# A new plan for the instruction order of an attention, MoE and SwiGLU kernel: transfer times, matmul kinds, a shared port, later gates, division on ACT too

## The chip, the cores and the metric

The kernel runs on one core of a Trainium2 chip. The metric is the device time of one execution in microseconds (us), lower is better. The engines are PE (TensorE, matmul and transposes), DVE (VectorE), ACT (ScalarE), POOL (GpSimd) and SP (SyncE, which here only issues DMAs).

## What is computed

All arrays are float32. Attention has batch 2, 8 heads, 576 tokens and head size 64, with a causal mask and a decay bias from a cumulative sum of s:

```python
cum = np.cumsum(np.maximum(s, 0.0), axis=-1)
bias = np.minimum(-(cum[..., :, None] - cum[..., None, :]), 0.0)
scores = np.where(causal, -1e9, q @ k.T / 8 + bias)
attn = np.exp(scores - scores.max(-1))
attn = attn / (attn.sum(-1) + 1e-09)
x = (attn @ v)                               # 1152 tokens x 512
p = domain_probs / (domain_probs.sum(-1) + 1e-09)
for e in range(4):                           # 512 -> 1024 -> 512
    y += p[:, e:e+1] * (np.maximum(x @ w1[e], 0) @ w2[e])
g = y @ w_gate                               # 512 -> 1536
out = (g * sigmoid(g) * (y @ w_val)) @ w_out
```

Each float32 matmul behind attention is made of three with split operands (high and low parts in the float32r format).

## The kernel before

**Stages.** Attention comes first, and dense work of the MoE is woven into it. The 16 pairs of heads times two parts of the sequence make 16 entries of `pairs`: pairs 0 to 7 are early (rows 0 to 255 of each head), pairs 8 to 15 late (rows 256 to 575). For each group of a pair, PE makes scores (L511, L516) with the mask added by a matmul (L519); DVE adds the decay bias and takes the row minimum (`least`, L533, since signs are turned); ACT takes the exponential with its sum (`exp`, L542); DVE adds 1e-9 and inverts (`guard`, L548, L549); one engine multiplies the row by that inverse (`norm`, through `scale`, L327: the division); PE transposes the result (`turn`, L587); ACT or DVE copies the transposes into p; PE multiplies by v (`products`, L646); and the result x is kept as a high and a low part (L662). The bias tile of an early pair, dqe, and the two of a late pair, dql and d, are fetched from a scratch array in DRAM, `rows`, to which the cumulative sum was written; pairs 0 and 1 get theirs through PE instead (`pick`, L451). There are three dqe buffers.

**The order.** Nothing is ordered by hand. All work is given to a planner (`Plan`) as tasks with an engine or a choice of engines, a cost in us, dependencies, buffers (`Ring`) and a rank. `Plan.step` takes the task that can start first by the planner's clocks, lowest rank among equals, and emits its instructions then. Each engine runs its instructions in the order emitted. The costs are constants at the top of the file: `COST` and `pe32` for engines, `ISSUE` and `DMA_KB` for a transfer's issue and its bytes, `DRAIN` and `SWITCH` for PE. They fix the order alone: the program waits for what really is not ready. While PE would be idle by the plan, `fill` puts transposes of a unit matrix there (L399, fillers).

**DMAs.** Almost all are issued by SP, in the planned order: k, q and v of the pairs, bias tiles, weights (`raw`, L784), and dps, the gate probabilities of the MoE (`gates`, L1462), which four small DVE operations (L1466 to L1469) normalise.

**Behind attention** (from about 143 us on) PE runs the rest of the MoE and then SwiGLU, with weights and activations split and added by ACT, DVE and POOL.

Of the kernel before, what the change touches and what calls it, by code (L numbers as in the profile page):

```python
# [17 lines left out]
P = 128  # L18
# [10 lines left out]
NSEL = 2  # L29
SWITCH = 0.15  # L30
NPT = 4
DRAIN = 0.3
HELD = 0.3
HELD2 = 1.0
# [9 lines left out]
AW = 1.6  # L44
NORM = "p"
COPY = "av"
# [13 lines left out]
ISSUE = 0.45  # L60
DMA_KB = 0.0028
SPLIT = "apv"
# [5 lines left out]
LOADS = 12  # L68
GRANK = 17
CUM2 = 10  # L70
CUMAT = 14.0
# [5 lines left out]
UMUL = "vp"  # L77
ULOW = "vp"
ENGINE = {"a": "act", "v": "dve", "p": "pool"}

# [34 lines left out]
def pe32(c):  # L115

    return 2 * max(c / 1200 + 0.003, 0.107)
# [7 lines left out]
class Ring:  # L125


    def __init__(self, n):
        self.n, self.ends = n, []
# [6 lines left out]
class Task:  # L136


    def __init__(self, eng, cost, run, deps, take, give, rank):
        self.eng, self.cost, self.run, self.take, self.give, self.rank = eng, cost, run, take, give, rank  # L140
        self.end, self.held, self.then, self.at, self.same = None, [], [], 0.0, {}
        if eng == "dma":
            self.cost, self.moves = cost
        self.missing, self.note = 0, None
        for d in deps:
            if d.end is None:
                self.missing += 1
                d.then.append(self)
            else:
                self.after(d)  # L150
# [10 lines left out]
class Plan:  # L161


    def __init__(self):
        self.clock = {e: 1.9 if e == "act" else 0.6 for e in ("pe", "act", "dve", "pool", "dma", "bus", None)}
        self.ready, self.filler, self.held = [], None, HELD

        self.busy, self.full = [0.0], [False]

    def add(self, eng, cost, run=None, deps=(), take=(), give=(), rank=0.0):  # L170
        t = Task(eng, cost, run, [d for d in deps if d is not None], take, give, rank)
        if not t.missing:
            self.ready.append(t)
        return t

    def start(self, t):

        at = t.at
        for i, r in enumerate(t.take):
            e = r.free(sum(x is r for x in t.take[:i]))  # L180
            if e is None:
                return None
            at = max(at, e + WAIT)
        if not isinstance(t.eng, dict):
            return max(at, t.same.get(t.eng, 0.0), self.clock[t.eng] if t.eng else 0.0), None
        best = None
        for e, cost in t.eng.items():
            x = max(at, t.same.get(ENGINE[e], 0.0), self.clock[ENGINE[e]])
            key = x + AW * cost + (self.held if e == "v" else 0.0)
            if best is None or key < best[0]:  # L190
                best = (key, x, e)
        return best[1:]
# [32 lines left out]
    def step(self, allow=lambda t: True):  # L225

        best = None
        for t in self.ready:
            if (best is None or t.at <= best[0][0]) and allow(t):
                x = self.start(t)  # L230
# [19 lines left out]
        if t.run:  # L250
            t.run(e) if e else t.run()
        t.end = self.run_pe(at, t.cost) if t.eng == "pe" else at + t.cost
        if t.eng == "dma":
            self.clock["dma"] = t.end
            t.end = self.clock["bus"] = max(t.end + 0.65, self.clock["bus"]) + t.moves
        elif t.eng:
            self.clock[t.eng] = t.end
# [13 lines left out]
def attention_moe_swiglu(ctx, tc, q_early, q_late, k, v, s, dp, w1, w2, wg, wv, wo, out):  # L271
# [40 lines left out]
    def any_of(engines, kind, c, run, deps, n=1, **kw):  # L312
        return add(choices(engines, kind, c, n), None, run, deps, **kw)

# [26 lines left out]
    def attention(ap, ps):  # L341
# [22 lines left out]
        def upper():  # L364
# [8 lines left out]
        spread2 = [(tri[lo, 0:P], mask[lo, :]), (tri[hi, lo], mask[hi, hi]), (tri[lo, P:], mask[lo, lo]), (tri[hi, P:], mask[hi, hi])]  # L373
        t_mask = [any_of("v", "copy", P, lambda e, x=x: move(e, *x), t_clear + [t], rank=-96.5)
                  for y, t in ((spread, t_id), (spread2, t_up)) for x in y]
# [45 lines left out]
        def prepare(pi, release):  # L421
# [24 lines left out]
            if pi < NSEL:  # L446
                def pick():
                    bias()
                    tp = ps.tile([P, BANK], F32, name="tp", tag="tp", bufs=2)
                    for j in range(2):  # L450
                        nc.tensor.matmul(tp[:, j * w:j * w + w], ident[:BH, BP * j + m:BP * j + m + 1].to_broadcast([BH, P]),  # L451
                                         sums[:, early], start=True, stop=True)
                    decay[pi, "tp"] = tp
                first = add("pe", 2 * pe32(w), pick, [t_early, t_id], take=[rg, ring("tp")], rank=rank)
                tb = [any_of("a", "bank", 2 * w, lambda e: move(e, decay[pi].rearrange("p j n -> p (j n)"), decay[pi, "tp"]), [first],
                             give=[(first, ring("tp"))], rank=rank - 60)]
            else:
                of = rows_e if exact else rows_l
                first = fetch(bias, lambda: of[m::BP, :w].partition_broadcast(P), 2 * w // 2, [release, t_rows[-1]], rank + 0.2, take=[rg])
                tb = [first]  # L460
            used[pi] = [(tq, ring(tag)), (first, rg)]
            if not exact:
# [16 lines left out]
            t_ready[pi] = [tk, tq, *t_mask], tb  # L479
        used = {}  # L480
        spent_v = {}
# [8 lines left out]
        def group(i, pi, ch, qbs):  # L490
# [67 lines left out]
            ready, bias = t_ready[pi]  # L558
            cost = sum(pe32(w) for _, _, w in segs) + (0.1 if two else 0.13 * len(segs) + SWITCH)
            tS = inorder("s", add("pe", cost, scores, ready + [before.get("s")], take=[rg] * 2, rank=i + RANK["s"]))  # L560
            exps, owner = [], {}
# [14 lines left out]
            for lane, heads in enumerate(lanes):  # L576
                r = i + lane * len(segs) + len(segs) - 1
                blocks = [(c, qb, at) for c in range(qbs[-1] + 1) for qb, at, w in segs if c <= qb]
                for c0 in range(0, len(blocks), BANK // P):
# [23 lines left out]
                    def copy(on, parts=parts):  # L603
                        for src, h, where in parts:
                            if h not in ch.p:
                                ch.p[h] = ap.tile([P, NB - 1, 320], F32, name="p", tag="p", bufs=NPT)
                            move(on, where(ch.p[h]), src)
                    cols = len(part) * P
                    tT = inorder("t", add("pe", len(part) * pe(2 * P) + 0.06, turn, norms[lane] + [before.get("t")], take=[ring("tp")],
                                          give=[(owner[lane], ring("ns"))] if c0 + len(part) == len(blocks) else [], rank=r + RANK["t"]))  # L610
# [9 lines left out]
        class Chunk:  # L620
# [30 lines left out]
            def values(self, i):  # L651
# [9 lines left out]
                def low():  # L661
                    nc.vector.tensor_tensor(xl[:, hp, dst], self.po[:, :n], f32(xh[:, hp, dst]), op=ALU.subtract)  # L662
                cost = DRAIN + sum(pe32(self.e - max(c * P, self.a)) for c in range(self.qbs[-1] + 1))
                tV = inorder("v", add(
                    "pe", cost, self.products,
                    self.done[0] + self.done[1] + [t_raw[pi, "v"], before.get("v")],
# [51 lines left out]
    class Narrow:  # L718
# [7 lines left out]
        def make(self, a):  # L726
# [38 lines left out]
            head = add("act", 0.67, one, [first], rank=rank)  # L765
            t3 = add("dve", 0.6, three, [head], rank=rank)
            t4 = add("act", 0.67, four, [head], rank=rank)
            t5 = add("dve", 0.9, five, [t3, t4], rank=rank)
            last = add("dve", 0.9, six, [t5], give=[(first, ring("r64"))], rank=rank)
            t = add("dma", (0.48, 0.73), store, [last], give=[(first, ring("n64"))], rank=rank)  # L770
# [689 lines left out]
    def gates(ap):  # L1460
        dps = ap.tile([P, NT, E], F32, name="dps", bufs=1)
        got = [add("dma", (ISSUE, 0.06), lambda: nc.sync.dma_start(dps, dp), rank=GRANK)]  # L1462

        def run():
# [31 lines left out]
    with ExitStack() as st:  # L1496
# [7 lines left out]
        late["made_n"] = 0  # L1504
        plan.held = HELD2
        rings["h"].n, rings["o"].n = 5, 3
# [69 lines left out]
```

## Time and profile before

| | |
|---|---|
| three runs | 727.9, 730.24, 727.9 us; median 727.9 |
| profiled execution | 727.63 us, span 725.8 us |
| busy in the span | PE 97%, PEld 84%, DVE 76%, ACT 47%, POOL 67% |
| mean granted TensorE clock | 0.99 of full speed |
| chain that ended last | PE 73%, DVE 11%, DMA 6%, issue 4% |
| DMA | 79.8 MB in 726 us |

The span is the time from the first to the last instruction of the profiled execution. Busy time counts an engine's instructions, overlaps once; PEld is the loading of matmul weights, which runs beside PE. A view of waits names the instruction that stood, the one that ended its wait, the sum, how often, and the longest. The chain of waits follows the last instruction back, step by step, to what released it.

### The profile page before, as it was taken

Reading aid. Unit: us, or ns where it says so; the run is one execution under the profiler, and the core shown is the slowest. Engines: PE = TensorE matmul, PEld = TensorE weight load, DVE = VectorE, ACT = ScalarE, POOL = GpSimd, SP = SyncE. Lnnn points to the kernel's source line nnn. Section 1 sums busy time; section 2 is a strip of 40 time slices with the busy share of each in tenths; the row PEclk is TensorE's granted clock in tenths of the full one; section 3 lists DMA queues with packets and bytes.
Section 4 is the critical chain, followed back from the end, with each engine's and each line's share of the span. In section 5 each row is a group of like instructions: output and inputs, shape, how many; then the busy total and the mean of one; then the engine's idle time right before and its main releaser. Section 6 shows DMA issues by size and latency. Waiting matters only on the chain.

```text
span 725.8 us, 11966 instructions
## 1 busy us (share of the span) xinstructions
PE 706.1 (97%) x4274; PEld 611.9 (84%) x4274; DVE 554.3 (76%) x1063; ACT 340.4 (47%) x729; POOL 484.4 (67%) x482
## 2 busy tenths in 40 slices
PE   7989999998999999999999999999999999999997
PEld 6766666687889888989899988998898999999996
DVE  5646666499268799999999999866866778787765
ACT  3755555523435445555555565555654324242210
POOL 2777463588646488547665876799899767685321
PEclk9899999999999999999999999999999999999999
DMA  5886562002114345454555454222121102010003
GB/s 141 261 251 200 152 192 89 30 30 88 52 65 145 145 126 194 146 179 129 173 172 189 143 178 146 88 87 88 30 67 51 59 30 75 32 40 1 1 1 130
DMA packets 31451, 79.78 MB, mean 110 GB/s; under 512 B 3568, under 2 KB 9216, under 8 KB 31392
## 3 DMA queue, kind: packets, MB, share of 16 engines
q1 hardware_dynamic: 31248, 78.90, 34.3%
q8 instruction: 33, 0.54, 0.3%
q14 instruction: 26, 0.21, 0.1%
q10 hardware_dynamic: 144, 0.13, 0.1%
HBM read 67.16 MB, written 11.85 MB: 109 GB/s over the span
## 4 chain that ended last, share of the span: by engine, by line
PE 73%; DVE 11%; DMA 6%; issue 4%; ACT 2%; POOL 2%; SPq 1%; DVEq 0%; POOLq 0%; ACTq 0%
PE o L1143 10%; PE o L1145 10%; PE o L1144 10%; PE h L1081 10%; PE h L1083 10%; PE h L1082 10%; PE po L646 3%; DVE tt L1020 3%; PE tp L587 2%; PE sp L516 2%; DMA dqe<-rows 2%; DMA d<-rows 2%; PE h L981 1%; DVE acc_a L1231 1%; DVE cc L1100 1%
## 5 line engine op out<-in xcount | busy, mean ns | idle before, releaser
L1143 PE MATMUL o<-woh,hh 128*128 128x512 f32 x396 | 157.6, 398 | 4.7 <-DVE acc_a L1231 3.0
L1100 DVE TENSOR_TENSOR cc<-cc,h 128x320 f32<-128x320 f32 (+1 forms) x282 | 124.7, 451 | 44.4 <-PE h L1083 38.5
L1145 PE MATMUL o<-woh,hl 128*128 128x512 f32 x396 | 155.1, 392 | 0.7 <-DVE hl L330 0.6
L1144 PE MATMUL o<-wol,hh 128*128 128x512 f32 x396 | 155.8, 393 | 0.0
L330 POOL TENSOR_TENSOR wal<-raw,wah 128x512 fp32r<-128x512 f32 (+1 forms) x58 | 70.6, 1225 | 39.5 <-ACT wah L317 36.2
L1081 PE MATMUL h<-xh,wsh 128*128 128x320 f32 (+1 forms) x312 | 93.0, 298 | 0.0
L1083 PE MATMUL h<-xh,wsl 128*128 128x320 f32 (+1 forms) x312 | 92.8, 297 | 0.0
L1082 PE MATMUL h<-xl,wsh 128*128 128x320 f32 (+1 forms) x312 | 92.7, 297 | 0.0
L1143 PEld LDWEIGHTS o<-woh,hh 128*128 128x128 f32 x396 | 74.5, 188 | 19.4 <-DVE acc_a L1231 4.1
L1145 PEld LDWEIGHTS o<-woh,hl 128*128 128x128 f32 x396 | 74.4, 188 | 18.8 <-DVE hl L330 1.7
L330 POOL TENSOR_TENSOR wol<-raw,woh 128x512 fp32r<-128x512 f32 x54 | 78.4, 1461 | 16.5 <-ACT woh L317 15.9
L1144 PEld LDWEIGHTS o<-wol,hh 128*128 128x128 f32 x396 | 74.5, 188 | 10.8
L330 POOL TENSOR_TENSOR hl<-cc,hh 128x512 fp32r<-128x512 f32 (+1 forms) x24 | 37.2, 1553 | 49.6 <-ACT hh L1203 48.9
L1081 PE MATMUL h<-xh,wah 128*128 128x320 f32 (+1 forms) x234 | 69.6, 297 | 0.7 <-DVE cc L1100 0.7
L1083 PE MATMUL h<-xh,wal 128*128 128x320 f32 (+1 forms) x234 | 69.4, 296 | 0.0
L1082 PE MATMUL h<-xl,wah 128*128 128x320 f32 (+1 forms) x234 | 69.3, 296 | 0.0
L327 POOL TENSOR_SCALAR ns<-ns,st 128x128 f32<-128x128 f32 (+3 forms) x72 | 39.2, 556 | 42.5 <-DVE st L549 34.3
L330 POOL TENSOR_TENSOR wsl<-sf,wsh 128x512 fp32r<-128x512 f32 x44 | 66.2, 1525 | 0.8 <-ACT wsh L317 0.8
L1200 ACT ACTIVATE cc<-cc 128x640 f32<-128x640 f32 (+1 forms) x46 | 32.0, 696 | 71.2 <-DVE cc L1100 70.8
L1081 PEld LDWEIGHTS h<-xh,wsh 128*128 128x128 f32 x312 | 58.9, 189 | 1.6
L1231 DVE SCALAR_TENSOR_TENSOR acc_b<-o,pr,acc_b 128x512 f32<-128x512 f32 x75 | 55.3, 742 | 6.4 <-PE o L1145 6.3
L1082 PEld LDWEIGHTS h<-xl,wsh 128*128 128x128 f32 x312 | 59.0, 189 | 1.4
(140 smaller groups left out, 1702.6 us busy)
## 6 DMA issues: line engine op xcount, KB each, us to landing
raw<-in_w SPq DMA_DIRECT2D x42, 512.0 KB, 5.1
n<-hl SPq DMA_DIRECT2D x36, 256.0 KB, 2.4
raw<-n SPq DMA_DIRECT2D x18, 512.0 KB, 3.4
hh<-in_wg SPq DMA_DIRECT2D x12, 512.0 KB, 4.5
hh<-in_wv SPq DMA_DIRECT2D x12, 512.0 KB, 4.4
hh<-in_wo SPq DMA_DIRECT2D x12, 512.0 KB, 3.9
dql<-rows SPq DMA_DIRECT2D x8, 512.0 KB, 5.6
vr<-in_v SPq DMA_DIRECT2D x4, 640.0 KB, 4.1
```

What stands on the lines that cost most here:

```text
L327: {"v": nc.vector, "p": nc.gpsimd}[e].tensor_scalar(to, x, by, 1.0, op0=ALU.mult, op1=ALU.mult)
L330: {"v": nc.vector, "p": nc.gpsimd}[e].tensor_tensor(to, x, f32(y), op=ALU.subtract)
L646: nc.tensor.matmul(po[half[j], lo - a:e - a], raw[self.pi // 2]["v"][:kn, c, two + j * D:two + j * D + D], self.spot(self.p[j], c, lo, e, ...
L1081: nc.tensor.matmul(hp, wh, h, start=c == 0, stop=False)
L1082: nc.tensor.matmul(hp, wh, l, start=False, stop=False)
L1083: nc.tensor.matmul(hp, wl, h, start=False, stop=c == 1)
L1100: nc.vector.tensor_tensor(part(k), part(x), banks[i], op=ALU.add)
L1143: nc.tensor.matmul(op, hh[:, f, ts], wh[:, f, :], start=f == 0, stop=False)
L1144: nc.tensor.matmul(op, hh[:, f, ts], wl[:, f, :], start=False, stop=False)
L1145: nc.tensor.matmul(op, hl[:, f, ts], wh[:, f, :], start=False, stop=f == NF - 1)
L1200: nc.scalar.activation(src()[:, o], src()[:, o], AF.Relu)
L1231: nc.vector.scalar_tensor_tensor(acc(t), bank_(), sc, acc(t), op0=ALU.mult, op1=ALU.add)
```

## The change

Numbers of the planner change, and what it knows of the machine grows. A transfer costs more per KB (`DMA_KB`), and 1.3 instead of 0.65 us pass between its issue and its bytes (`LANDING`). A task of PE has a kind of matmul (`mode`), and a change of kind costs `CHANGE`, in place of `SWITCH` and parts of other costs. Some operations of DVE ("two", "copy" and "scale", not those that read PSUM) and those of POOL share a port by the plan, and there never overlap while attention is planned (`port`, `ported`). `HELD` goes to 0, so DVE is no longer held back as a choice. Two things change beside the costs: the division may run on ACT too (`NORM`), as may the copies that build the mask; and the fetch of dps is not to start before 24 us of the plan (`GATES`). Fetches of bias tiles keep the order of their pairs (`chain_d`).

```diff
-SWITCH = 0.15
-DRAIN = 0.3
-HELD = 0.3
+DRAIN = 0.1
+HELD = 0.0
-NORM = "p"
+NORM = "pa"
-DMA_KB = 0.0028
+DMA_KB = 0.0033
+GATES = 24.0
+CHANGE = 0.09
+LANDING = 1.3
+PORTED = {"dve": "v", "pool": "p"}
...
-            return max(at, t.same.get(t.eng, 0.0), self.clock[t.eng] if t.eng else 0.0), None
+            x = max(at, t.same.get(t.eng, 0.0), self.clock[t.eng] if t.eng else 0.0)
+            return max(x, self.clock["port"]) if self.ported and t.eng in PORTED and PORTED[t.eng] in t.port else x, None
...
+        if t.eng == "pe":
+            t.cost += CHANGE * (t.mode != self.mode)
+            self.mode = t.mode
         t.end = self.run_pe(at, t.cost) if t.eng == "pe" else at + t.cost
+        if t.eng in PORTED and PORTED[t.eng] in t.port:
+            self.clock["port"] = t.end
         if t.eng == "dma":
             self.clock["dma"] = t.end
-            t.end = self.clock["bus"] = max(t.end + 0.65, self.clock["bus"]) + t.moves
+            t.end = self.clock["bus"] = max(t.end + LANDING, self.clock["bus"]) + t.moves
...
-        return add(choices(engines, kind, c, n), None, run, deps, **kw)
+        return add(choices(engines, kind, c, n), None, run, deps, port="vp" if kind in ("two", "copy", "scale") else "p", **kw)
...
-        t_mask = [any_of("v", "copy", P, lambda e, x=x: move(e, *x), t_clear + [t], rank=-96.5)
+        t_mask = [any_of("av", "copy", P, lambda e, x=x: move(e, *x), t_clear + [t], rank=-96.5)
...
-                first = fetch(bias, lambda: of[m::BP, :w].partition_broadcast(P), 2 * w // 2, [release, t_rows[-1]], rank + 0.2, take=[rg])
+                first = fetch(bias, lambda: of[m::BP, :w].partition_broadcast(P), 2 * w // 2, [release, t_rows[-1], chain_d.get(tag)], rank + 0.2, take=[rg])
                 tb = [first]
+            chain_d[tag] = first
...
         got = [add("dma", (ISSUE, 0.06), lambda: nc.sync.dma_start(dps, dp), rank=GRANK)]
+        got[0].at = GATES
...
-        plan.held = HELD2
+        plan.held, plan.ported = HELD2, False
```

What this makes of the order shows best at three places. In these listings a row is an instruction (or several alike), with its line, what it writes and reads, and its size; the lines of the changed program are 10 to 12 higher. Across both programs PE's matmuls are the same but for fillers, 50 instead of 44; of the 72 divisions ACT takes 50, and POOL keeps 22.

The first place is SP's queue from the sums' rows (rows_104) to the second bias tile dqe, with the semaphores that each issue waits for; DMAHW0 to 7 are told by landings of DMAs. Before:

```order
L358 DMA rows_104<-sums 16x256 [waits DVE_49]
L358 DMA dqe<-rows_104 128x2x256 [waits DMAHW7_49,DMAHW0_49]
L358 DMA k_109<-in_k 128x256 [waits DMAHW1_49]
L358 DMA qe<-in_q_early 128x256 [waits DMAHW2_49]
L358 DMA vr<-in_v 128x512 [waits DMAHW3_49]
L358 DMA vr<-in_v 128x512 [waits DMAHW4_49]
L358 DMA rows_105<-sums 16x576 [waits DMAHW5_49,DVE_49]
L358 DMA k_110<-in_k 128x256 [waits DMAHW6_49]
L1462 DMA dps<-in_dp 128x36
L358 DMA k_111<-in_k 128x256 [waits DMAHW0_49]
L358 DMA dqe<-rows_104 128x2x256 [waits DMAHW1_49,DVE_49,Activation_49]
```

and in the changed program, where k_109 stands ahead of these rows:

```order
L368 DMA rows_104<-sums 16x256 [waits DMAHW0_49,DVE_49]
L368 DMA qe<-in_q_early 128x256 [waits DMAHW1_49]
L368 DMA vr<-in_v 128x512 [waits DMAHW2_49]
L368 DMA vr<-in_v 128x512 [waits DMAHW3_49]
L368 DMA k_110<-in_k 128x256 [waits DMAHW4_49]
L368 DMA dqe<-rows_104 128x2x256 [waits DMAHW5_49,DMAHW0_49]
L368 DMA rows_105<-sums 16x576 [waits DMAHW6_49,DVE_49]
L368 DMA k_111<-in_k 128x256 [waits DMAHW7_49]
L795 DMA raw<-in_w 128x1024
L368 DMA dqe<-rows_104 128x2x256 [waits DMAHW1_49,DVE_49,Activation_49]
```

The first dqe moved behind a q, two v and a k, and the fetch of dps is gone from here; it now stands 19 places later, behind the last early dqe, a late k and a late q.

The second place is DVE around the four gate operations. Before, they stand in the middle of pair 1's minima (h), ahead of the guard of its first head:

```order
L533 ISA ns,st<-h,dqe 128x256
L533 ISA st 128x1
L1466 TENSOR_REDUCE sm<-dps 128x9
L1467 TENSOR_SCALAR sm<-sm 128x9
L1468 RECIPROCAL sm<-sm 128x9
L1469 TENSOR_TENSOR pr<-dps,sm 128x36
L548 TENSOR_SCALAR st<-st 128x2
L549 RECIPROCAL st<-st 128x2
L533 ISA ns,st<-h,dqe 128x128
```

and now between the minima of pair 6 and those of pair 7:

```order
L544 ISA ns,st<-sp,dqe 128x256
L544 ISA st 128x1
L329 CAST xh<-po 128x256
L559 TENSOR_SCALAR st<-st 128x2
L560 RECIPROCAL st<-st 128x2
L1478 TENSOR_REDUCE sm<-dps 128x9
L1479 TENSOR_SCALAR sm<-sm 128x9
L1480 RECIPROCAL sm<-sm 128x9
L1481 TENSOR_TENSOR pr<-dps,sm 128x36
L673 TENSOR_TENSOR xl<-po,xh 128x256
L544 ISA ns,st<-sp,dqe 128x128
```

The gates moved behind five more pairs, and a cast of x stands on DVE that ACT had before.

The third place is ACT at the early pairs 6 and 7. Before, exponentials (L542) alternate with copies of transposes and casts of x:

```order
L542 ACTIVATE ns,st<-ns,st 128x128
L542 ACTIVATE ns,st<-ns,st 128x256
L317 CAST xh<-po 128x256
L317 COPY p<-tp 128x384 x2
L542 ACTIVATE ns,st<-ns,st 128x128
L542 ACTIVATE ns,st<-ns,st 128x256
```

and in the changed program divisions (L335) stand between the exponentials (L553):

```order
L553 ACTIVATE ns,st<-ns,st 128x128
L335 ACTIVATE ns<-ns,st 128x128
L553 ACTIVATE ns,st<-ns,st 128x256
L553 ACTIVATE ns,st<-ns,st 128x128
L327 COPY p<-tp 128x384
L335 ACTIVATE ns<-ns,st 128x128
L553 ACTIVATE ns,st<-ns,st 128x256
L335 ACTIVATE ns<-ns,st 128x256
```

ACT got the divisions that POOL had, and gave copies to DVE.

## Rows read from the trace of the kernel before

**Rows 1.** The page's first part: busy time, share of the span, instructions

```profile
PE 706.1 (97%) x4274; PEld 611.9 (84%) x4274; DVE 554.3 (76%) x1063; ACT 340.4 (47%) x729; POOL 484.4 (67%) x482
```

**Rows 2.** Windows, the fillers (L399) alone: window, PE and PEld busy, clock, DMA

```profile
8.40:68.10 59.70, 5.48 (x30) 4.55 (x30) 0.89 0.79 230
```

**Rows 3.** Waits, whole span: who waited for whom, us in total, times, longest

```profile
POOL d L476 <- DMA d<-rows: 13.6, 5, 4.5
DVE sm L1466 <- DMA dps<-in_dp: 4.3, 1, 4.3
PE tp L587 <- POOL ns L327: 3.5, 2, 2.0
PE o L1143 <- DVE acc_a L1231: 3.0, 3, 1.6
PE h L516 <- DVE st L533: 2.6, 1, 2.6
PE h L1081 <- DVE cc L1100: 2.1, 2, 1.4
```

**Rows 4.** Windows, busy of PE, PEld, DVE, ACT, POOL, then clock, DMA share, GB/s

```profile
26.70:42.50 15.80, 14.79 (x143) 11.74 (x141) 11.22 (x57) 13.40 (x51) 10.86 (x21) 1.00 0.87 224
...
79.10:90.40 11.30, 11.30 (x73) 7.65 (x72) 6.59 (x24) 6.33 (x18) 3.54 (x6) 1.00 0.55 162
```

**Rows 5.** Timeline of DVE: start, us, instruction, [idle before it and what ended that]

```profile
15.25 0.19 DVE L1466 TENSOR_REDUCE sm<-dps 128x9 f32<-128x36 f32 x1 [4.34 <-DMA dps<-in_dp]
...
19.96 0.29 DVE L533 CUSTOM_DVE_ANT_0 ns<-h,dqe 128x128 f32<-128x128 f32 x1 [0.94 <-PE tp L587]
...
26.75 0.29 DVE L533 CUSTOM_DVE_ANT_0 ns<-sp,dqe 128x128 f32<-128x128 f32 x1 [1.64 <-DMA dqe<-rows]
```

**Rows 6.** The chain that ended last, 0 to 80 us: start, us, what

```profile
4.80 1.41 DMA rows<-sums
...
6.72 6.28 DMA k<-in_k
...
13.07 6.49 DMA dqe<-rows
...
19.64 6.95 DMA dqe<-rows
```

**Rows 7.** Timeline of SP's queue: start of the issue, us, transfer

```profile
6.30 0.38 SPq L358 DMA_DIRECT2D dqe<-rows  x1
...
10.11 0.43 SPq L1462 DMA_DIRECT2D dps<-in_dp  x1
12.62 0.33 SPq L358 DMA_DIRECT2D k<-in_k  x1
```

**Rows 8.** Timeline of ACT, the first exponential of a late group

```profile
47.73 0.62 ACT L542 ACTIVATE ns<-ns,st 128x384 f32<-128x384 f32 x1
```

**Rows 9.** The DMA view of 19.6 to 26.6 us

```profile
DMA packets 1605, 2.42 MB, mean 346 GB/s; under 512 B 140, under 2 KB 1310, under 8 KB 1603
```

**Rows 10.** Groups by line and shape, ACT: busy us, mean ns, idle before it

```profile
L317 ACT COPY p<-tp 128x384 f32<-128x384 f32 x32 | 14.3, 477 | 8.2 <-PE tp L587 7.9
...
L542 ACT ACTIVATE ns<-ns,st 128x256 f32<-128x256 f32 x16 | 8.0, 503 | 0.1
...
L542 ACT ACTIVATE ns<-ns,st 128x128 f32<-128x128 f32 x16 | 6.4, 400 | 5.9 <-DVE st L533 5.8
```

**Rows 11.** The chain again, at the first dense matmuls behind attention matmuls

```profile
69.12 0.43 PE o L1143
69.54 0.23 PE o L1144
```

**Rows 12.** Timeline of DVE and POOL: a free guard, and one beside POOL

```profile
16.05 0.16 DVE L548 TENSOR_SCALAR st<-st 128x2 f32<-128x2 f32 x1
...
32.08 1.27 POOL L330 TENSOR_TENSOR wol<-raw,woh 128x512 fp32r<-128x512 f32 x1
32.35 1.02 DVE L548 TENSOR_SCALAR st<-st 128x2 f32<-128x2 f32 x1 [0.15 <-ACT ns L542]
```

More of the change, by code (lines that the diff above doesn't have):

```diff
@@ L136, with __init__ @@
 class Task:
-    def __init__(self, eng, cost, run, deps, take, give, rank):
+    def __init__(self, eng, cost, run, deps, take, give, rank, port, mode):
+        self.port, self.mode = port, mode
         self.eng, self.cost, self.run, self.take, self.give, self.rank = eng, cost, run, take, give, rank
@@ L164, in __init__, with add @@
     def __init__(self):
-        self.clock = {e: 1.9 if e == "act" else 0.6 for e in ("pe", "act", "dve", "pool", "dma", "bus", None)}
-        self.ready, self.filler, self.held = [], None, HELD
+        self.clock = {e: 1.9 if e == "act" else 0.6 for e in ("pe", "act", "dve", "pool", "dma", "bus", "port", None)}
+        self.ready, self.filler, self.held, self.mode, self.ported = [], None, HELD, "r", True
         self.busy, self.full = [0.0], [False]
-    def add(self, eng, cost, run=None, deps=(), take=(), give=(), rank=0.0):
-        t = Task(eng, cost, run, [d for d in deps if d is not None], take, give, rank)
+    def add(self, eng, cost, run=None, deps=(), take=(), give=(), rank=0.0, port="p", mode="r"):
+        t = Task(eng, cost, run, [d for d in deps if d is not None], take, give, rank, port, mode)
         if not t.missing:
@@ L184, in start @@
         if not isinstance(t.eng, dict):
-            return max(at, t.same.get(t.eng, 0.0), self.clock[t.eng] if t.eng else 0.0), None
+            x = max(at, t.same.get(t.eng, 0.0), self.clock[t.eng] if t.eng else 0.0)
+            return max(x, self.clock["port"]) if self.ported and t.eng in PORTED and PORTED[t.eng] in t.port else x, None
         best = None
         for e, cost in t.eng.items():
-            x = max(at, t.same.get(ENGINE[e], 0.0), self.clock[ENGINE[e]])
+            x = max(at, t.same.get(ENGINE[e], 0.0), self.clock[ENGINE[e]], self.clock["port"] if self.ported and e in t.port else 0.0)
             key = x + AW * cost + (self.held if e == "v" else 0.0)
@@ L453, in pick @@
                     decay[pi, "tp"] = tp
-                first = add("pe", 2 * pe32(w), pick, [t_early, t_id], take=[rg, ring("tp")], rank=rank)
+                first = add("pe", 2 * pe32(w), pick, [t_early, t_id, chain_d.get(tag)], mode="s", take=[rg, ring("tp")], rank=rank)
                 tb = [any_of("a", "bank", 2 * w, lambda e: move(e, decay[pi].rearrange("p j n -> p (j n)"), decay[pi, "tp"]), [first],
@@ L479, in prepare @@
             t_ready[pi] = [tk, tq, *t_mask], tb
-        used = {}
+        used, chain_d = {}, {}
         spent_v = {}
@@ L558, in group @@
             ready, bias = t_ready[pi]
-            cost = sum(pe32(w) for _, _, w in segs) + (0.1 if two else 0.13 * len(segs) + SWITCH)
-            tS = inorder("s", add("pe", cost, scores, ready + [before.get("s")], take=[rg] * 2, rank=i + RANK["s"]))
+            cost = sum(pe32(w) for _, _, w in segs) + (0.1 if two else 0.13 * len(segs))
+            tS = inorder("s", add("pe", cost, scores, ready + [before.get("s")], mode="f" if two else "s", take=[rg] * 2, rank=i + RANK["s"]))
             exps, owner = [], {}
@@ L608, in group @@
                     cols = len(part) * P
-                    tT = inorder("t", add("pe", len(part) * pe(2 * P) + 0.06, turn, norms[lane] + [before.get("t")], take=[ring("tp")],
+                    tT = inorder("t", add("pe", len(part) * pe(2 * P), turn, mode="f", deps=norms[lane] + [before.get("t")], take=[ring("tp")],
                                           give=[(owner[lane], ring("ns"))] if c0 + len(part) == len(blocks) else [], rank=r + RANK["t"]))
@@ L664, in values @@
                 tV = inorder("v", add(
-                    "pe", cost, self.products,
+                    "pe", cost, self.products, mode="c", deps=
                     self.done[0] + self.done[1] + [t_raw[pi, "v"], before.get("v")],
@@ L765, in make @@
             head = add("act", 0.67, one, [first], rank=rank)
-            t3 = add("dve", 0.6, three, [head], rank=rank)
+            t3 = add("dve", 0.6, three, [head], port="v", rank=rank)
             t4 = add("act", 0.67, four, [head], rank=rank)
-            t5 = add("dve", 0.9, five, [t3, t4], rank=rank)
-            last = add("dve", 0.9, six, [t5], give=[(first, ring("r64"))], rank=rank)
+            t5 = add("dve", 0.9, five, [t3, t4], port="v", rank=rank)
+            last = add("dve", 0.9, six, [t5], port="v", give=[(first, ring("r64"))], rank=rank)
             t = add("dma", (0.48, 0.73), store, [last], give=[(first, ring("n64"))], rank=rank)
```

## Prediction

> **What bounds the kernel now.** I read the page's first part, then the waits of PE, then the chain of waits, and then the first 70 us instruction by instruction, since that is the stretch that the planner's new costs order anew. PE is busy for 706.1 of 725.8 us [rows 1], and the matrix work that has to be done is the same in both programs. So time can come only from PE time that does no work: idle, filler transposes, half clock, drains. Most of it lies early. Between 8.4 and 68.1 us PE runs 30 fillers that take 5.5 us, at a mean granted clock of 0.89 [rows 2], and its two largest waits (3.5 us for normalised heads from POOL, 2.6 us for DVE [rows 3]) lie there too. From 79.1 to 90.4 us, one whole late pair, PE is busy 11.30 of 11.30 us [rows 4]: the late pairs are PE-bound, with that period.
>
> Why is PE empty early? Two things stand side by side. **First**, DVE waits 4.3 us for the gate probabilities, dps [rows 3], until 15.25 us [rows 5], with the guards of pair 1, its other minima and pair 2 queued behind. **Second**, the chain of waits goes through DMAs: k (from 6.72 us, 6.28 long), the second dqe (13.07, 6.49), the third (19.64, 6.95) [rows 6]. Each is tied to the next through SP. A transfer has one of eight semaphores, and SP issues it only when the one eight places before has landed (the waits on DMAHW0 to 7 in the order listings). So SP stands after dps, issued at 10.11, until 12.62, when the first dqe of 6.30 has landed [rows 7]. The second dqe lands at 13.07 + 6.49 = 19.56, and pair 3's first minimum starts at 19.96; the third lands at 26.59, and pair 4's starts at 26.75 [rows 5, 6]. Taking away the dps wait alone would therefore free pairs 1 and 2, but give only some 0.4 us at pair 3: the DMA chain stands right behind it.
>
> After that ACT is the limit, 13.40 busy of 15.80 us from 26.7 to 42.5 [rows 4]. Then POOL waits for a bias tail (five such waits, 13.6 us in all [rows 3]) with the last early heads queued behind it, and the first exponential of a late group starts at 47.73 us [rows 8].
>
> **The change, part by part.** *DMA order.* The first dqe now goes behind a q, two v and a k. These and the sums' rows are five issues of some 0.45 us [rows 7]; the rows went out at 4.80 [rows 6] and go a little earlier now, so dqe leaves near 6.9 instead of 6.30. The second dqe has that q eight places ahead of it, not the k that landed at 13.00; it waits instead for its buffer, free when pair 0's four minima are done, well before 13. The third waits for the first to land: it took 12.62 - 6.30 = 6.3 us [rows 7], so 6.9 + 6.3 = 13.2. With 6.95 us of its own it is there at 20.1 instead of 26.59: **-6.5 us** for pair 4.
>
> *Gates.* dps moves 19 places down SP's queue, behind the last early dqe and two late loads (k and q, 352 KB), and its four small DVE operations move to between pairs 6 and 7. Removed is a wait of 4.3 us where DVE has work; whatever of it counts is in the 6.5 already. Added: dps lands after those 352 KB, about 1 us behind the last dqe at the 346 GB/s that ran from 19.6 to 26.6 us [rows 9], and pair 7's minima stand behind it. I cost it at 0, because ACT still has pair 6's exponentials then; without that cover it is 1 us.
>
> *Division on ACT.* ACT takes 50 of the 72 divisions. From pair 4's first exponential to the first late one its order holds 9 of 128 and 6 of 256 columns. No row of before shows one; nearest is the exponential of the same shape, 400 and 503 ns [rows 10], of which neighbours overlap by some 90: 9 x 0.31 + 6 x 0.41 = 5.3 us. Against that, 4 copies of 477 ns [rows 10] and 3 casts of x go to DVE: 4 x 0.38 + 3 x 0.27 = 2.3. Net +3.0 us on the engine that limits this stretch. The stretch took 42.5 - 26.75 = 15.75 us, 2.4 of them idle on ACT [rows 4]. So it ends between 20.1 + 13.4 + 3.0 = 36.5, where the idle time absorbs all, and 20.1 + 15.75 + 3.0 = 38.9. I take the later, since ACT must now wait for guards as well. The last early heads no longer stand in POOL's queue behind the bias tail, so the late exponentials follow at once, near 39 instead of 47.73: **-8.7 us**. Their loads hang on pair 3's products, which come 6.5 us earlier too.
>
> *Repaid on PE.* At that point the new order has about one products group and two groups of transposes more still to do: **+1.0 us**. In the late pairs dense work comes in three pieces instead of two. The first matmul after attention takes 0.43 us, the next 0.23 [rows 11]; six pairs with one more such step: **+1.2 us**. For ACT standing before a guard I add **+0.5 us** (0 where another exponential is ahead in the queue; 0.2 for each of the 15, 3.0, where none is; nearer to none, by ACT's 85% load in rows 4).
>
> *Fillers, mask casts, the rest.* Six more fillers at 5.5 / 30 = 0.18 us fill time that is empty in any case (1.1 us if it is not). The four casts on ACT lie beside the load of s, before ACT has other work. Behind attention PE's order is the same but for a few matmuls that change places with transposes; what DVE and POOL do there is dealt out a little differently. 0, with bounds of 3 us either way, the size of PE's largest wait there [rows 3].
>
> Sum: -8.7 + 1.0 + 1.2 + 0.5 = **-6.0 us**. The profiled execution took 727.63 us, 1.8 over its span and 0.3 under the median of the runs, 727.9. Forecast: **721.6 us**. Under 0.5% (3.6 us) can hardly be told from no change here.
>
> **Rivals.** *A, slower: ACT becomes the limit of the late pairs.* Its 6.33 us of work in a period of 11.3 [rows 4] gets 3.6 divisions of about 0.6 us and loses some 0.5 of copies: 8.0. If it stands for guard, reciprocal and three hand-overs before each, about 0.7 us by estimate, that is 2.5 more. And a guard waits for POOL: at 32.35 one took 1.02 us instead of 0.16 and ended 0.02 us after the POOL operation of 1.27 us that began before it [rows 12]; 3.6 of these, 3.1 more. All of it gives 13.6. It decides from 11.3 upward, and so needs nearly every wait. At 13.1 it is 721.6 + 8 x 1.8 = **736 us**. For it: ACT's queue is in order. Against: the dense pieces leave several us between scores and transposes. Chance 0.10.
>
> *B, the loads in front eat the gain.* A dqe behind 768 KB of q, v and k starts its data 2.2 us later at 346 GB/s, and each 512 KB of weights ahead of the second and third adds 1.5 [rows 9]. The third then lands at 22.3 to 25.3, and the time is **723.8 to 726.8 us**. Against: the third dqe's 6.95 us already had two such weights before it. In the Trainium skill, "DMA: Bandwidth & Descriptors", section "Queues, rings and completion order", each DMA engine consumes the descriptors of a ring in their order. That rule speaks for B, and against an order that puts loads ahead of what is waited for; the chain's landings agree with it as far as they go. Chance 0.16.
>
> *C, the elementwise work behind attention falls worse.* PE waits there for DVE in many small pieces, the two largest groups 3.0 and 2.1 us [rows 3]. Doubled: 721.6 + 5.1 = **726.7 us**. For: DVE and POOL have new orders there. Against: PE's order is the old one. Chance 0.12.
>
> *D, more than forecast.* ACT's idle time absorbs its new work (36.5 instead of 38.9), the 0.5 goes, and the 3.5 us for which PE waited for POOL's heads go too: 721.6 - 2.4 - 0.5 - 3.5 = **715.2 us**. Chance 0.12.
>
> **How the numbers follow.** The forecast, 717 to 725, has 0.50; A 0.10, B 0.16, C 0.12, D 0.12. Faster by over 0.5% is below 724.0: 0.46 of the forecast, all of D, 0.04 of B, 0.02 of C, together 0.64. Slower is above 731.3: 0.09 of A and 0.03 of C. The rest, 0.24, is within. The range from 714 to 729 leaves out A, the worst part of C and the lower tail of D, under 2 in 10.
>
> **What would show it.** Right: no DVE wait for dps before pair 7; pair 4's minima near 20 us; the first late exponential near 39; a late period of still about 11.3 us with PE full; less idle and filler time before 60 us, the same idle after 140. Wrong: dqe landings as late as before (B); ACT over 90% busy from 60 to 130 us with PE waiting for it (A); new PE waits for DVE after 180 us (C).

## The result, and the profile after

The changed kernel takes 718.32 us (median, 717.22 to 720.01) against 727.9 us before: a ratio of 0.9863, 95% interval 0.9834 to 0.9893. The forecast was 721.6 us with a range of 714 to 729, so the sign held and the time lies in the range, 3.3 us under the forecast. Several steps on the way there did not hold, and two large misses cancelled. Ratios and intervals are the record's estimate over all executions, and can differ a little from the quotient of two medians.

The page's first part, for the changed kernel, beside [rows 1]:

```profile
PE 698.9 (97%) x4280; PEld 607.2 (85%) x4280; DVE 557.2 (78%) x1081; ACT 358.2 (50%) x757; POOL 463.2 (65%) x436
```

The waits of the changed kernel over the whole span (who waited for whom, us in total, times, longest), beside [rows 3]:

```profile
ACT ns L335 <- DVE st L560: 15.4, 24, 1.7
...
DVE st L559 <- ACT ns L553: 9.8, 20, 1.1
...
POOL d L487 <- DMA d<-rows: 9.3, 4, 7.6
...
PE tp L598 <- ACT ns L335: 1.7, 3, 0.9
PE o L1156 <- DVE hl L340: 1.7, 1, 1.7
...
PE o L1154 <- DVE acc_a L1242: 1.6, 2, 1.3
PE o L1270 <- DVE xl L1281: 1.5, 1, 1.5
```

The 3.5 us for POOL's heads and the 2.6 us for DVE early on are gone, and so is DVE's wait for dps. ACT now waits 15.4 us for DVE's reciprocals, since it divides; PE feels 1.7 us of waits for ACT's heads. DVE's wait of 9.8 us for ACT's exponentials is not new, it was longer before:

```profile
DVE st L548 <- ACT ns L542: 13.5, 19, 1.5
```

POOL's wait for bias tails fell from 13.6 to 9.3 us. Behind attention PE's waits are other and somewhat smaller ones (1.7, 1.6 and 1.5 us against 3.0 and 2.1 in [rows 3]).

Windows of the changed kernel (busy PE, PEld, DVE, ACT, POOL, clock, DMA share, GB/s), from the first minimum of pair 4 to the first late exponential, and over five late pairs, beside [rows 4]:

```profile
22.30:43.20 20.90, 18.83 (x164) 14.56 (x162) 16.45 (x71) 16.49 (x59) 13.26 (x17) 1.00 0.82 241
62.30:118.20 55.90, 55.77 (x361) 37.06 (x360) 36.96 (x124) 41.84 (x100) 17.21 (x23) 1.00 0.50 161
```

A late pair still takes 55.90 / 5 = 11.2 us with PE full, and ACT is at 75%. The fillers alone, beside [rows 2]:

```profile
8.40:68.10 59.70, 4.53 (x32) 3.63 (x32) 1.00 0.79 230
```

DVE's timeline, beside [rows 5]; its lines are those of pair 3, pair 4 and the gates:

```profile
17.95 0.29 DVE L544 CUSTOM_DVE_ANT_0 ns<-h,dqe 128x128 f32<-128x128 f32 x1 [1.19 <-DMA dqe<-rows]
...
22.29 0.29 DVE L544 CUSTOM_DVE_ANT_0 ns<-sp,dqe 128x128 f32<-128x128 f32 x1 [2.19 <-POOL wal L340]
...
35.31 0.17 DVE L1478 TENSOR_REDUCE sm<-dps 128x9 f32<-128x36 f32 x1
35.52 0.92 DVE L1479 TENSOR_SCALAR sm<-sm 128x9 f32<-128x9 f32 x1
```

Pair 3 starts 2.0 us earlier than before, pair 4 4.5 us (forecast 6.5). ACT's first late exponential, beside [rows 8], comes at 43.25 instead of 47.73; the forecast was 39:

```profile
43.25 0.60 ACT L553 ACTIVATE ns<-ns,st 128x384 f32<-128x384 f32 x1
```

**A ledger of PE's time.** To compare the kernels I walked PE's instructions up to the point where 6.8% of the dense columns are done. Attention is behind it in every order, so the work up to there is the same. PE takes some 133.2 us for it in both kernels, and between 131 and 135 in the variants below, where it is ordered another way. What the point comes later than 133.2 + 1.65 us (PE's first instruction) is lost time: gaps, fillers, and half the time spent at half clock on real work. It is 20.6 us before, at 155.4 us, and 14.5 us after, at 149.3 us. That is 6.1 us, where the forecast said 6.0; the agreement is luck, as the steps show. From there to the last dense matmul another 2.5 us are gained. In what follows "lost" is this number. It is read from the one profiled execution of a kernel, which can lie 2.5 us from the median of its times.

### The profile page after: what moved, and what is told of

Same layout as the page of the kernel before. It is cut to its first block, busy times and chain, and to the rows that moved or that the text cites. A ratio compares the mean times of both kernels' runs of the same rounds, so it can differ in the third digit from the quotient of the medians.

```text
span 717.2 us, 11928 instructions
## 1 busy us (share of the span) xinstructions
PE 698.9 (97%) x4280; PEld 607.2 (85%) x4280; DVE 557.2 (78%) x1081; ACT 358.2 (50%) x757; POOL 463.2 (65%) x436
## 4 chain that ended last, share of the span: by engine, by line
PE 74%; DVE 12%; POOL 5%; issue 4%; ACT 4%; DMA 0%; DVEq 0%; ACTq 0%; POOLq 0%
PE h L1092 10%; PE h L1094 10%; PE h L1093 10%; PE o L1154 10%; PE o L1155 10%; PE o L1156 10%; PE tp L598 2%; PE po L657 2%; PE sp L527 2%; DVE tt L1031 1%; ACT ns L553 1%; PE h L992 1%; DVE cc L1111 1%; PE h L994 1%; PE h L993 1%
## 5 line engine op out<-in xcount | busy, mean ns | idle before, releaser
L340 POOL TENSOR_TENSOR wol<-raw,woh 128x512 fp32r<-128x512 f32 x54 | 79.2, 1475 | 15.0 <-ACT woh L327 14.5
L340 POOL TENSOR_TENSOR hl<-cc,hh 128x512 fp32r<-128x512 f32 (+1 forms) x28 | 41.9, 1498 | 52.8 <-ACT hh L1214 52.6
L1094 PEld LDWEIGHTS h<-xh,wsl 128*128 128x128 f32 x312 | 59.0, 189 | 0.0
```

The source lines that it names most:

```text
L340: {"v": nc.vector, "p": nc.gpsimd}[e].tensor_tensor(to, x, f32(y), op=ALU.subtract)
L1094: nc.tensor.matmul(hp, wl, h, start=False, stop=c == 1)
```

## Experiments

Each was timed beside the kernel before on the same chip. The time of each is its median; ratios are to the kernel before. Experiments 6, 7, 8 and 10 ran on another chip than 11 and 12, where the changed kernel was timed again, so differences of theirs to the changed kernel go across chips (the kernel before took 728.72 and 728.58 us on the two). A changed constant makes the planner deal out all engines anew; only 2, 4, 9 and 10 keep an order.

**1. The gates alone.** On the kernel before:

```diff
+        got[0].at = 24.0
```

> The kernel before, with the gates' load put off (at = 24.0) and nothing else. Theory (the DMA chain stands right behind the dps wait): DVE's 4.3 us wait for dps goes, but pair 3's first minimum still starts at 19.5 to 20.0 and pair 4's near 26.6, the first late exponential at 46.5 to 48; time 727.5 us, between 726 and 729. Rival (the dps wait is what held the early stretch): the first late exponential near 43.5, time 723.5.

730.85 us, ratio 1.0028 (1.0 to 1.0056); lost 22.7 us. The wait for dps at its old place is gone, and DVE waits for the second dqe instead. Its timeline, and SP's queue ahead of that load:

```profile
21.27 0.29 DVE L533 CUSTOM_DVE_ANT_0 ns<-h,dqe 128x128 f32<-128x128 f32 x1 [5.93 <-DMA dqe<-rows]
```

```profile
12.55 0.33 SPq L784 DMA_DIRECT2D raw<-in_w  x1
13.05 0.38 SPq L358 DMA_DIRECT2D dqe<-rows  x1
```

dps left its place in the queue, and a 512 KB weight came in ahead of dqe, which now took 8.1 us instead of 6.49 [rows 6]. The rival falls, but the theory's numbers were too good as well: pair 3 starts at 21.27, the first late exponential stands at 49.13, and the time is 730.85. It did not ask what moves into a free place.

**2. dps moved up the queue, nothing else.** Every engine's order is the recorded one of the kernel before; SP's list has dps ahead of the sums' rows and the first dqe.

```diff
-q, rows, dqe, k, q, v, v, rows, k, dps, k, dqe
+q, dps, rows, dqe, k, q, v, v, rows, k, k, dqe
```

> The kernel before with every engine's order as it was, but the gates' load moved up SP's queue, ahead of the sums' rows and the first dqe. Theory (behind the dps wait stands the DMA chain, as the prediction has it): DVE's 4.3 us wait for dps goes, pair 3's and pair 4's first minima stay at 19.5 to 20.5 and 26.3 to 27, and the time is 726.5 to 728.5. Rival (the wait is a limit of its own; it cost more than 3 us only where the planner dealt the rest out anew): 723 to 725.

728.28 us, ratio 0.9998 (0.997 to 1.0026); lost 19.2 us. DVE's timeline:

```profile
13.66 0.18 DVE L1579 TENSOR_REDUCE sm<-dps 128x9 f32<-128x36 f32 x1
...
25.37 0.29 DVE L646 CUSTOM_DVE_ANT_0 ns<-sp,dqe 128x128 f32<-128x128 f32 x1 [2.60 <-DMA dqe<-rows]
```

No wait for dps, pair 4 still waits for its dqe, and the time is the old one. This is the cleanest test of the prediction's claim that the DMA chain stands right behind the dps wait: a DVE wait of 4.3 us was worth nothing that could be told (the interval allows some 2 us either way). The profiled execution is one of the faster ones, 725.91 us. In it pair 4 starts 1.4 us earlier than in the kernel before, outside what was expected, and the first late exponential stands at 45.37.

**3. The measured transfer times alone.** On the kernel before, with the gates early and division on POOL:

```diff
-DMA_KB = 0.0028
+DMA_KB = 0.0033
-            t.end = self.clock["bus"] = max(t.end + 0.65, self.clock["bus"]) + t.moves
+            t.end = self.clock["bus"] = max(t.end + 1.3, self.clock["bus"]) + t.moves
```

> The kernel before, with the measured transfer times alone (0.0033 us per KB and 1.3 us to land, for 0.0028 and 0.65); its gates still load early and DVE still waits for them. Theory (the order of the loads is the change): the third dqe lands near 22 instead of 26.59, the first late exponential at 41 to 44, time 722 to 724. Rival (the waits on DVE and POOL hold the stretch, the loads are hidden): within 1 us of the kernel before.

719.24 us, ratio 0.9894 (0.9846 to 0.9941); lost 15.0 us. Two constants of the planner bring most of the change's gain. DVE even keeps its wait for dps, PE stands 4.3 us for DVE there, and the first late exponential comes 3.0 us earlier than before:

```profile
17.48 0.19 DVE L1466 TENSOR_REDUCE sm<-dps 128x9 f32<-128x36 f32 x1 [3.61 <-DMA dps<-in_dp]
```

```profile
PE h L516 <- DVE st L533: 4.3, 1, 4.3
```

```profile
44.73 0.62 ACT L542 ACTIVATE ns<-ns,st 128x384 f32<-128x384 f32 x1
```

The third dqe landed at 24.02, not the 22 that was expected, and the late exponentials came later than the 41 to 44; yet the time is better than the 722 to 724. So the theory is not borne out as it stood. Against the kernel before, the first late exponential comes 3.0 us earlier, the ledger's point 5.6 and the last dense matmul 8.6.

**4. The order of the loads alone.** Again every engine's recorded order of the kernel before; SP's first 31 loads go in the order that the changed planner gives with early gates.

```diff
-q, rows, dqe, k, q, v, v, rows, k, dps, k, dqe, q, raw, k, raw, raw, q, k, dqe, dqe
+q, k, rows, q, v, v, k, dps, dqe, rows, k, raw, dqe, q, raw, k, raw, dqe, q, k, dqe
```

> The kernel before with every engine's order as it was (replayed from a record), SP's alone changed: its first 31 loads go in the order of the changed planner with early gates, so k, q and v and then dps go ahead of the first dqe, and each later dqe goes one to three places earlier. Theory (the order of the loads is what gains): DVE has dps by about 10 us and does not wait for it, the second dqe lands near 18 instead of 19.6 and the third near 23 instead of 26.6, the first late exponential at 44 to 45.5, time 722 to 725. Rival (PE, DVE and ACT need an order planned for those landings): 726 to 728.5.

724.82 us, ratio 0.9953 (0.9928 to 0.9979); lost 18.2 us. The third dqe landed at 23.34, the first late exponential stood at 45.01; the second dqe landed at 19.45, not near 18. The time is the theory's, but its gain is only about a third of what the change gains. The rest must come from the order of PE, DVE, ACT and POOL, or of the later loads; which of them is not shown.

**5. Division alone.** On the kernel before:

```diff
-NORM = "p"
+NORM = "pa"
```

> The kernel before, with division on ACT or POOL (NORM = "pa") and nothing else. Theory (in the old order the early stretch hangs on DMA, and after it on ACT): +1 to +3 us, 729 to 731, first late exponential at 47.5 to 50. Rival (heads that stand in POOL's queue behind a bias tail are the loss, and ACT takes them out of it): PE's waits for POOL's heads (3.5 us) go and the late pairs start near 44; 723 to 725.

731.79 us, ratio 1.0062 (1.0036 to 1.0089); lost 24.0 us. Two of PE's waits, the first its largest:

```profile
PE tp L587 <- ACT ns L325: 3.6, 3, 1.5
...
PE tp L587 <- ACT p L317: 2.2, 4, 1.2
```

The wait for POOL's heads, 3.5 us before, became one of 3.6 us for ACT's, and the copies that ACT owes came late as well. The rival falls.

**6. Division back on POOL.** On the changed kernel:

```diff
-NORM = "pa"
+NORM = "p"
```

> The changed kernel with division on POOL alone (NORM = "p") and nothing else. Theory (the forecast's terms: division put 3.0 us on ACT, 1.2 us of extra steps and 0.5 us of waits on guards; and alone it made the kernel before slower): 714 to 717. Rival (in the new order POOL would be the limit, and PE waits for its heads again): PE's waits for ns from POOL come to 3 us or more, time 720 to 723.

715.77 us, ratio 0.9818 (0.9779 to 0.9857); lost 9.8 us. DVE's timeline, ACT's first late exponential, and the windows from the one to the other and of the late pairs:

```profile
20.99 0.29 DVE L544 CUSTOM_DVE_ANT_0 ns<-sp,dqe 128x128 f32<-128x128 f32 x1 [1.81 <-DMA dqe<-rows]
```

```profile
40.15 0.62 ACT L553 ACTIVATE ns<-ns,st 128x384 f32<-128x384 f32 x1
```

```profile
20.99:40.15 19.16, 19.16 (x174) 15.29 (x171) 15.29 (x71) 13.38 (x49) 15.32 (x28) 0.97 0.83 255
62.30:118.20 55.90, 54.98 (x378) 37.41 (x376) 36.57 (x120) 32.28 (x87) 30.19 (x43) 1.00 0.44 144
```

Pair 4 starts at 20.99 and the late exponentials at 40.15. That is nearly what the prediction had for the whole change (20.1 and 39). With division on ACT they come at 43.25, 3.1 us later. Of these, 1.3 us are there at pair 4 already, and the stretch itself is 1.8 us longer (20.96 against 19.16), though ACT does some 3 us more in it (16.49 against 13.38 busy). PE's work up to the ledger's point is 131.4 us here, so 1.8 of the 4.7 us of lost time between the two are work that became shorter. The late pairs are PE-bound either way, though ACT has 9.6 us less to do in them.

**7. Gates early again.** On the changed kernel:

```diff
-GATES = 24.0
+GATES = 0.0
```

> The changed kernel with the gates' load back at its early place (GATES = 0.0) and nothing else. Theory (once the loads are in the new order, the dps wait is no longer covered by the DMA chain): DVE waits 3 to 4 us for dps again, pair 3's guards start at 19 to 21 instead of 17.95, and the time is 719 to 722. Rival (the gates are a side matter in either order, as they were alone): 717.5 to 719, no difference that can be told.

716.22 us, ratio 0.9816 (0.9774 to 0.9858); lost 11.3 us. Both the theory and the rival fall. The wait does not come back, because dps now goes out ahead of the first dqe, at 6.71. SP's queue, and DVE's timeline:

```profile
6.71 0.43 SPq L1473 DMA_DIRECT2D dps<-in_dp  x1
```

```profile
11.94 0.19 DVE L1478 TENSOR_REDUCE sm<-dps 128x9 f32<-128x36 f32 x1
12.16 0.17 DVE L1479 TENSOR_SCALAR sm<-sm 128x9 f32<-128x9 f32 x1
```

So the new order is faster with early gates. In the changed kernel the operations of the late gates lie on the chain of waits:

```profile
35.39 0.10 DVE sm L1478
...
35.52 0.93 DVE sm L1479
...
36.47 0.23 DVE sm L1480
```

From 35.39 to 36.78 the chain runs through the gates, 1.4 us. But these are not what the variant gained, for its first late exponential is no earlier than the changed kernel's 43.25:

```profile
43.81 0.62 ACT L553 ACTIVATE ns<-ns,st 128x384 f32<-128x384 f32 x1
```

Its profiled execution has 3.2 us less lost all the same. PE simply has more to do early, in the window in which the changed kernel keeps it busy for 18.83 us:

```profile
22.30:43.20 20.90, 20.02 (x172) 14.74 (x172) 16.14 (x68) 19.01 (x68) 15.76 (x21) 1.00 0.85 244
```

What part the gates have in that is open; the planner dealt out all engines anew here too.

**8. The old transfer times again.** On the changed kernel:

```diff
-DMA_KB = 0.0033
+DMA_KB = 0.0028
-LANDING = 1.3
+LANDING = 0.65
```

> The changed kernel with the old transfer times in its planner (0.0028 us per KB, 0.65 us to land) and nothing else. The loads keep nearly the same order (the second and third dqe go out a place or two earlier), since each dqe is now also tied to the one before it; what is dealt out around them is new. Theory (what counts is the order in which the dqe loads go): third dqe lands at 21 to 23, time 717 to 720. Rival (what counts is that PE's and DVE's order is planned for loads that land late): 722 to 726.

716.45 us, ratio 0.9828 (0.9789 to 0.9866); lost 15.5 us. The third dqe landed at 21.55. The rival falls: the other new rules bring the loads into a good order without the new times. Either way is enough. Which of the rules does it (the order of the dqe fetches, the matmul kinds, the shared port, `HELD`) is not shown, since none was changed alone.

**9. Fillers doubled.** On the kernel before, in `keep_on`, orders as they were:

```diff
+            for _ in range(2):
                 nc.tensor.transpose(idle["p"][:, :P], ident, ident)
```

> The kernel before in its own order, each filler transpose issued twice. It asks what the stretches at half clock (13.6 us, 10.9 of them with real work on PE) cost. Rival (the clock is most of what the change gained over the forecast): at least two of the three stretches are granted full clock and the time is 722.5 to 724. Theory (early PE work waits for loads and ACT in any case): whatever the clock does, 726.5 to 728.5.

726.91 us, ratio 1.0 (0.9975 to 1.0025); lost 22.7 us. The three stretches in the kernel before, and in this one:

```profile
7.80:11.20 3.40, 3.40 (x27) 3.18 (x24) 2.18 (x14) 2.46 (x11) 0.83 (x2) 0.51 0.50 104
18.10:24.90 6.80, 6.80 (x41) 5.41 (x38) 3.41 (x21) 3.61 (x15) 4.58 (x10) 0.50 1.00 367
45.40:48.80 3.40, 3.40 (x20) 2.65 (x18) 1.04 (x4) 1.59 (x5) 2.95 (x5) 0.50 0.64 158
```

```profile
7.80:11.20 3.40, 3.40 (x38) 2.85 (x38) 1.48 (x8) 1.81 (x5) 0.00 (x0) 1.00 0.32 95
18.10:24.90 6.80, 5.29 (x52) 3.90 (x49) 3.50 (x21) 5.39 (x22) 4.04 (x9) 1.00 0.98 356
45.40:48.80 3.40, 3.14 (x18) 2.56 (x18) 1.04 (x4) 1.43 (x4) 3.40 (x5) 0.70 0.38 90
```

The clock came back in two of the three, half-clock loss fell from 5.5 to 0.3 us, fillers rose from 8.1 to 13.5, and the time did not move. (The profile is of the slowest of its ten executions, 728.68 us.)

**10. No fillers.** On the changed kernel, in `keep_on`, its order kept:

```diff
-            nc.tensor.transpose(idle["p"][:, :P], ident, ident)
```

> The changed kernel in its own order without the 50 filler transposes (8 us of PE). Up to the point where 6.8% of the dense columns are done, PE loses 14.4 us in the changed kernel (gaps 6.5, fillers 8.0, half clock 0) and 20.7 in the kernel before (7.1, 8.1, 5.5). Theory (the waits set that sum, and how it splits into idle, filled and half-clock time counts for little): gaps grow to 10 to 14, half clock to 1 to 5, sum 14 to 16.5, time 718 to 720.5. Rival (the clock is what counts): most of the first 45 us at half clock, sum over 19, time 723 or more.

719.62 us, ratio 0.9858 (0.9812 to 0.9904); lost 15.0 us. Where the trace holds a clock record, it shows half clock from 23.6 to 30.5 us; it holds none before 13.4 us. There the same score matmuls took 724 ns instead of 418 (groups of PE by shape, 5 to 13 us, without fillers and then in the changed kernel):

```profile
L526 PE MATMUL sp<-k,qe 64*128 64x256 f32 x6 | 2.0, 724 | 0.0
```

```profile
L527 PE MATMUL sp<-k,qe 64*128 64x256 f32 x8 | 1.4, 418 | 0.0
```

So half clock did come back, and fewer gaps than expected. The sum is the theory's, and 8 us of filler less left the time where it was.

**11. and 12. The two best edits together, and the changed kernel again beside them.** On the changed kernel, and for the second run no edit:

```diff
-NORM = "pa"
+NORM = "p"
-GATES = 24.0
+GATES = 0.0
```

> The changed kernel with the gates early (GATES = 0.0) and division on POOL alone (NORM = "p"). Each alone took some 2 us off the changed kernel. Theory (they free different time: a wait on loads, and work on ACT): 712 to 715. Rival (both live off the same lost PE time in the first 50 us, of which some 8 us is filler that no order removes): 715 to 717.5.

> The changed kernel itself, unedited, on the same chip as the runs beside it. If 717 to 720, the 2 us that its variants with early gates, with division on POOL and with the old transfer times are faster is real. If 715.5 to 717, it is scatter between chips.

714.34 us (713.52 to 715.73), ratio 0.9801 (0.9769 to 0.9833), lost 9.7 us; and 718.17 us (717.49 to 720.89), ratio 0.9858, lost 13.8 us. No run of the one is as slow as the fastest of the other, so 3.8 us over the changed kernel are real, as the theory had it, and near the sum of the two (2.4 and 2.0, measured on another chip). In these two profiled executions the first late exponential stands at 41.15 and 42.44. The version with the planner's new costs, but without late gates and without division on ACT, is the best one measured.

## Why the prediction was right, and where it was not

- **DMA order, the main term.** Right in direction: pair 4 started earlier because its load landed earlier, and experiment 2 shows the dps wait to be worth nothing that could be told while the chain of loads stands behind it. In size it gave 4.5 of 6.5 us at pair 4. The step that failed is "With 6.95 us of its own it is there at 20.1". The load was issued at 13.77 instead of 13.2, since the first dqe took 6.85 us and not 6.3, and it took 8.4 us of its own, so it landed at 22.13, just short of rival B's 22.3. SP's queue, the time to landing, and the DMA view of that stretch, beside [rows 9]:

```profile
13.77 0.58 SPq L368 DMA_DIRECT2D dqe<-rows  x1
```

```profile
DMA to landing us min/median/max: 8.4/8.4/8.4
```

```profile
DMA packets 1642, 2.43 MB, mean 290 GB/s; under 512 B 144, under 2 KB 1356, under 8 KB 1641
```

As many bytes moved while it was under way as in the 7 us of [rows 9] (2.42 MB), but at 290 instead of 346 GB/s. Why the rate was lower is open. A load that stands behind more bytes is late as well: in experiment 1, with one weight put ahead of a dqe, it was 8.1 us long instead of 6.49. In the Trainium skill, "DMA: Bandwidth & Descriptors", section "Queues, rings and completion order", a ring's descriptors are consumed in order; those two numbers agree with it.
- **From the late exponentials to the time.** The prediction carried a lead at the first late exponential over to the time one for one, less 2.7 us on PE. The runs do not bear that out. Experiments 3 and 4 have it at 44.73 and 45.01, and take 719.24 and 724.82 us; experiment 7 has it at 43.81, later than the changed kernel, and is faster. B's landing nearly came, but not its 723.8 us. And the order of the loads by itself gave 3.8 us (experiment 4). How much of the rest is better transfer times, and how much a lucky deal of the other engines, no run tells: experiments 1 and 5, dealt out anew as well, lost 3 and 4 us.
- **Gates.** That the removed wait is worth little was right. Whether the cost of 0 for the late place was right is open: dps itself was in time, landed at 31.01 and used at 35.31, and the four operations stand on the chain for 1.4 us there, but experiment 7 does not show those 1.4 us as time gained.
- **Division on ACT.** The +3.0 us of work on ACT was near in size: from pair 4's first minimum to the first late exponential ACT is busy for 16.49 us, against 14.2 before and 13.38 with division back on POOL. But that stretch is 21.0 us long in the changed kernel and 21.0 before. The step that failed is that the late exponentials "follow at once" after 15.75 + 3.0 = 18.75: it took 2.2 us more. ACT stood for 4.4 us in it, 3.5 of these for DVE's reciprocals, where the forecast had 2.4 us of idle time in all. So -4.5 instead of **-8.7 us**.
- **Repaid on PE.** +1.0, +1.2 and +0.5 did not come. PE's work up to the ledger's point is 133.2 us in both kernels, and from the late start to there it gained a further 1.6 us. The extra dense step per pair is there only against division on POOL, where the work is 131.4 us. This error of 4.3 us cancels the one of 4.2 us before it, by luck.
- **Behind attention.** 0 was forecast with 3 us either way; it gained 2.5, in steps of about 1 us up and down. DVE and POOL are dealt out differently there, but which step has which cause stays open. Rival C went the other way. By sum PE's second largest wait before was the 3.0 us for DVE there [rows 3], not the 2.6 that the prediction names; no term rests on it.
- **Rivals A and D.** ACT is busy 41.84 of 55.90 us in the late pairs, 8.4 a pair, where A's own work was put at 8.0; its waits of another 5.6 were not added to a chain that PE felt. D's 715.2 us was not reached; that division back on POOL takes 715.77 is another kernel and no test of D.

## What to carry to other kernels

Before pricing a wait that is taken away, look for the next arrival behind it: here a 4.3 us wait of DVE was worth nothing, because a load landed right after it. Transfer times of the trace, issue to landing, are a good first thing to give a planner: they brought 8.5 us to the old plan, though nothing to the new one, which does without them. Then test each hand-made rule again in the new order, since two that came with this change cost it nearly 4 us. Do not take one early mark, here the first late exponential, for the time. Compare kernels by time lost up to the same point of work; idle time, filler and half clock turn into each other.

## What the runs showed of the hardware

The granted clock early on was not worth what it seemed. The ledger puts 5.5 of the 6.1 us to half clock that is gone, but a run of the same changed kernel had half clock again in one stretch, at a time of 717.94 us in that execution (window of 7.8 to 11.2 us):

```profile
7.80:11.20 3.40, 3.40 (x25) 2.72 (x24) 1.84 (x11) 2.45 (x8) 0.00 (x0) 0.77 0.76 164
```

The execution shown above, whose profile has full clock throughout (1.00), took 719.07. In experiments 2 and 4, whose profiles hold no clock record before 14 us, the early score matmuls took 701 ns each, where 8 of 12 took 418 in the kernel before (PE by shape, 5 to 13 us, with dps moved up and before); neither was slower for it:

```profile
L629 PE MATMUL sp<-k,qe 64*128 64x256 f32 x4 | 1.2, 701 | 0.0
```

```profile
L516 PE MATMUL sp<-k,qe 64*128 64x256 f32 x8 | 1.4, 418 | 0.0
```

With experiments 9 and 10 that speaks for PE's early time being set by what it waits for.

A DVE operation on 9 elements a row, one of the late gates, took 0.92 us at 35.52, and 0.17 us in experiment 7 where POOL stood idle. POOL's timeline in the changed kernel:

```profile
35.12 1.28 POOL L340 TENSOR_TENSOR wol<-raw,woh 128x512 fp32r<-128x512 f32 x1
```

It ended within 0.05 us of that operation's end, as with the guard of [rows 12]. In the Trainium skill, "SBUF — State Buffer", section "SBUF: two separate sides", one port pair of DVE and POOL is locked for a whole instruction; this trace agrees with it.
